# Rows of nine tokens, and the two heads of P side by side, in a thresholded attention with a maxout network behind it

## The chip, the core and the metric

The kernel runs on one core of one Trainium2 chip. A core has five engines that each work through their own list of instructions: TensorE (PE, matmuls; its weight loads are listed apart as PEld), VectorE (DVE), ScalarE (ACT), GpSimd (POOL) and SyncE (SP), which here only issues DMAs. Sixteen DMA engines move the data. The metric is the time of one execution on the device in microseconds (us). Lower is better.

## The reference, cut to what matters

```python
# q, k, v: (8 batches, 8 heads, 576 tokens, 64), float32; tau = 0.02
scores = q @ k.T / 8
thresh = max(scores, axis=-1) - tau
scores = where(scores >= thresh, scores, -1e9)
attn   = exp(scores - max(scores)); attn = attn / sum(attn)
x      = (attn @ v), heads side by side        # (4608 tokens, 512)
h      = maximum(x @ w1, x @ w2, x @ w3)       # 512 -> 768
out    = h @ w_out                             # (4608, 512), float32
```

Every token attends only to the keys whose score is within tau of the row's maximum. Then a maxout network with three input matrices is applied to each token.

## The kernel before, in words

**Tiling.** A batch has eight heads. Four heads are a *quad* (16 quads in all), in the code `g` or `L`; a quad is two *pairs*, `r` = 0 and 1, of two heads `i` each. A head's 576 tokens are 64 groups of nine; a load puts the group on the partition, so a partition holds tokens that follow each other in DRAM. For q and k one transfer brings tokens 0 to 7 of each group (`qm`, `km`: 16 token columns for two pairs) and another one, once per batch, token 8 of all eight heads (`q9`, `k9`, in `nine`). V comes as `vm` in two transfers per quad, four tokens of four heads each, and its ninth tokens in `v9`.

**Transposes and scores.** PE transposes q and k two token columns at a time (`couple`, `transposed`, tile `tp`); ACT or DVE copies the result into `qt` and `kt`, which hold 320 columns for pair 0 and 256 for pair 1. POOL makes `qs`, which is `qt` with its two row halves exchanged (`swapped`). `scores` makes 128 query rows by 576 keys of one head as two matmuls, each in one 64-row half of PE (tile `sc`). A *chunk* is 128 query rows of one head of each pair; its two steps are the two pairs. There are 9 chunks in a quad, 144 in all.

**Softmax.** For each step DVE finds the row maximum (`maximum`, tile `z`), ACT applies the threshold and the exponential (`exponents`, `numerators`), for some steps DVE masks instead of ACT (the digits 1 and 3 in `MASKED`). DVE takes the reciprocal of the two sums of a chunk (`reciprocals`, tiles `sm`, `rs`), and POOL multiplies and writes P in bfloat16 (`normalized`): step 0 into columns 0 to 575, step 1 into columns 576 to 1151. A DMA transpose (`turned`) turns P into `ptq`, nine blocks of 128 keys.

**Product.** `product` multiplies `ptq` by V (`vb`, V cast to bfloat16 by POOL in `cast_v`). Each pair accumulates in its own PSUM bank. Since P of the two steps follow each other, a block of 128 rows of `ptq` mixes keys: in a first half of the work each pair uses one row half of PE, and in the second half (letter `D` in the order, `issue(1)`) the row halves are exchanged. A gate, an empty instruction that waits for the end of the first half, stands between the two.

**Network.** `ffn` has 9 hidden pieces per batch with three matrices (tiles `ph`, `hm`, `hT`), and the output pieces (`po`, copied into `ob`). `outp` stores an `ob` of 128 rows with one DMA: 14 stores of 512 KB for pairs of token columns, 4 of 256 KB for the last batch; `ninth` stores the ninth tokens of two batches, 4 of 256 KB. These pieces use both row halves of PE and are cut in two in the same way (`halves`).

**Order.** Nothing is scheduled at run time. The string `ORDER` names each step by a letter, in one global order, and `_Ordered` ties every engine's instructions to that order. The letters that matter here: `l` a load, `t` a DMA transpose, `o` an output store, `i` a store of ninths, `S` scores, `T` transposes, `O` a product, `D` its second half, `F` and `B` the halves of a network piece, `p` one step of P, `r` a reciprocal, `y` a cast of V. A digit behind `S`, `T`, `O`, `F` names the PSUM slot. All DMAs but three at the start are issued from SP, in the order of their letters, so SP's queue carries loads, transposes of P and stores in one line. Buffers: six for P, two for `ptq`, two for `ob`, two for loaded q, k and V.

Line 100 of the kernel is the call inside `_Ordered`, so nearly all instructions of the profile stand under L100; they are told apart by their tiles.

Of the kernel before, what the change touches and what calls it, by code (L numbers as in the profile page):

```python
# [11 lines left out]
F32 = mybir.dt.float32  # L12
# [9 lines left out]
FLAT = 2.0 ** -100  # L22

MASKED = """
223222232233222220210000021233202222122020000010000001011211000010000131
101030100000110000000100000110000001001112002102100000103000100101000100
000001100101100010001000001100100001000101010001100000001000001000010001
100001110010001010010100000100010000100111000100100100000000010001010000
# [4 lines left out]
150605614372873482158427036045238761134628750738260415253670418765830142  # L33
123687540257136804843612507412875036125083746786120435601505613782473842
# [14 lines left out]
lllllllT3laT0qT2CT3laqClqS1qmyeS3S2mS0mS1gnlenelmT3mAS2zgqgeenT3kgymCT0llS1gAerT3qlqS0mqpcrnpeS2gnmS1lnmprtp  # L49
S3etemppzS0emS1nlktmS2nrpememyrkS3epS0epnS2pS1kntmrtmrmepeeS0S2mbsnmpnS3leS1pmrmepS2S3penmnmO10semsrkzDsS3wS  # L50
2pdwnT1S0rpmlpAlsmeT3etpteqnS1mT0nercpAS3ppeS2emtS0nnyelS1memgnqrekpnmmS3eO21kDT0tkrpmdwneqnS2etpqrppzwnS1tc
tlrS0F3plpmmeprnBelF2mHbzBgvepS1nS0nmT3S2rmaetmeS1mF3kBnptdpteeF0S1vrBmT2S3phpeS0cmmnypS2nrmpnS1nsmdrS3ggF0e
BmszespnlO12vebnpsrpDnS0wF3S1epwS2mgT0zatqmmetttrpBenvqsT1tF0pqS2BqcnF1S3hepksgeBS0mmnrsF2S3evmspmdlpS1mBdnr
evnS3pS0mpO12ebdnrplmnS3zeDenplmlwS0twtrympetS3eS1etypelmyF2S3kmrBnmklF1pF0selT3kkBBAuhF2rtS1peS3ventnBmF0S1
mBvtpdrF3kepS2plsnBqmrhmT1eCvdS0S2pplmreT1danmS3mpnS0mpS1edreppddqF2eqF3npmT0eBkncqBeS1vF0S2HerBmelnmvS3F2em
pT1prkBltaT0S3vCS1tmS2plpnemmT3adS0S1O23qrkepstenmeeDmS1pkkrkS0xS2psxF3rmmttnpS1msS0S2pedenrtekenttpBmmumdnp
S1S0S2trmyeO13pslmpdpT0emnlteekcDS2rslrplpwS0S1mxetdqqketF3F2mmeBBnS0hF1kT3sqBmndaF0vS3dltppvrS2pmnlS1mBleF3
endS2mBepnyHF1nrqmF0vBtdrrpS2vneT3psCpBS1mnetpteF3HS2mBF1meS0nseF2sBBkvS3emvqpdsryhtmpyS0F1S2eF3tnepnemrBBmS
0pnvrpyvO12seDpmnkdekrS0xweT3T2pmpnS1pS0CpAlmF3tdqmlS2rsBS0mF1pHsnmeS2qF3prntnoBopemvBdeS0nrpdF2pS1vS3mBeF0l
etmS1nByemhltdrptknmF2eT3BvptS1rvaemeS0mnpeeS3mtkpF2nkS0snF3sretS1merBmpkUS1erBmppplnS0eS1qmtdtunO23mkqoeeS1  # L60
eDmrS0pnwpT1mxT3yppdndS2CperN0nApmldT3pS1cemnF2qBjS3tBdrnlltqkmS1yeeF0mS3nseHmntrdBF1olvrpF2BepBhS0S3vlF1S2B
mepmmeS3T0vnlF2pdT1eBpaS0rpmCkvdS1teF3dmetlmS2BnpmnprS0F1kS2mmrhqBdS3epepnF0ntdF2dvBetmS1vBT3pmtqS0npS1rkdht
aO23mlrS0qppdeeenmeDkmS1xkrmF0wT2plBeF1vpCdlnS2rnneqBmvS3edtpplS0F2pS1mmmBtdrinpS3lhF0eT1mBpadneS3dypnkvF1em
S2rBlpmS0dF3vS2tneBmmpF1rpHS0qpT2ttneBmrsF3tnS0dCsBvmvS1mS2pemS0epetednemqnF3T1etBkT2lCnnArUpS1edmeS0eeO23np
rdS1pkmkmDprlwwF0S1deserlkmS2epBpymF1S3qBeqrukmkhtdpS2S0mtnptF1nmS3BeF2pmrnvndF0ltdBrpS3T1teavpBemS2F1pHeqmp
S3msrdpnF0qS2mpBlF3vneBBrddtenvhedF2S1S0BkS3etemF1lemvT0BpmyCnntpS2tF3F0llrvymppS1nskBsBhyprmpvtS2S1mmdT0S3n
lmS2epaerkO01pS3mmpsesesDnnqeF3lewrF2qBT0ewF1reCyvkBBplnF3HnvS0pS2neBmovF1T0ttmsprBknS3ladhpmpS2F0mS1odrleyB
tmnesF3ptplT2BtS1qepvS0CvmmS2S3ndmrenF1eS0nkprpeT2mBmS3AqrdmT0eplpnF2cS3S0skeuepemtS1rdnmBeS3mpknueqS1mN0npt
S2mBT3pstjdrmtS1prekmAO20pedqkerdnS1nDmS3pslprdxxmoS1T2eF0mS3epqncnelpBF1mtHnS2mprssttBF3pT0apveS2BF0S1rnmpe
vdBmS2eS3HlpF1dennmmyprS0meBqepvF2tS3BmF0lvS1F3mBtBkF2dnnehdS1pvF0temsBrT3dqentdBvrHpF1pCeS2myenBlnvtS3pyF0s  # L70
mS2pmkBnslO13S2rrvemDsppS2F0qlwntepeemewnF1BrtdpBokT3tnhvpleaS2S0eS1mF3S2emBtF0rnpdmmvS1eT2BF3msS1pltnBqkypr
ChdsF2mytS0BnrS1letvlmevnqS3pS0mpptmpmeF2edS3kertnpelsS1F0BmT3empnS1enlkkskrBupmaT2pcS3S1uqdrerO02pemeS3kDmn
snmS3tqrpppS1wxlenF0trS2dpmnemS3lBF1lpeypmlmS2dT3hopyklameBS0F2vsrS3pBpmtF1smeveS0nBF3mttntlheS2kremBdT0evF1
F2pBcpvF3BrkendhBestvS0F1nmT2kqrF3aBBehppvrpdtS2mdS0ntS3pmmF1peeeS2BmtvO03S2nndkpenS1rDxmpmS2F1wrT3mS0nqBtdc
F2pesprS3nqmS0BqenvpedmmphF1T3aBT2CS0tvS3qeT1psmnF2dnmrepoekAF0prBBhvF3nS1BmsqF2tveqS0dBdperqS1eS3ptepmvmnnp
S0F2T1CmmS3rkntS0S1esBmrpsntepmpumS3eF0tS2tmmpkS1erBdkenpUO23nDmekrxS0epoN1wsmpteS2BjmnpS3rF0seF2tBBhpmkdS1F
3nndF0ovtBrmS2S1veepmtBF3kS2edhBeemspmF0F1rnpBlF2vpsS3rnBevkdtS0mplBhF1dvrS3mnmeBnseF2F0neBvhS3rpppF1nBpBmpF
3nF2dBevnvHpS0eS1tsmrmF3BeS0isS1rnvmdeBF2evtmptF0ntBF3BpnshrBpS1enyekvS2vpS0mmdtF3ymS1mdrBpnerO20S1neeDuS3mp
xxtenpO21mkpstDrS3xwesS2mnF0iemstF1BpptoF2pBkF3BerpnsnurtF0enBHF1BvrhBpF2vF0ptpvBF1BBpvptptF2BHvvO13O20DxDF1
uxowwF2F0oF1UBhF2BF0vBvF3BoBF1F2BhBvHF3F0BvBvvN3F0F1UouBjoi  # L80
# [31 lines left out]
def kernel(  # L112
# [58 lines left out]
    nines = {}  # L171

    def nine(b):
        if b not in nines:
            nines[b] = {n: ld.tile([128, 6 if n == "v" else 4, D], F32, name=n + "9", bufs=1) for n in "qkv"}
        return nines[b]

    def load(g, first=False):
        b, qd = quads[g]
        L = Ls[g] = dict(b=b, qd=qd, first=first)  # L180
        for n in "qk":
            L[n] = ld.tile([128, 16, D], F32, name=n + "m")
        L["vm"] = ld.tile([128, 4, 4, D], F32, name="vm")

        def rows_of(src, heads):
            return src[b, heads].rearrange("(r i) (p c) d -> (i p) r c d", i=2, c=9)

        four = slice(4 * qd, 4 * qd + 4)
        q2 = nc.scalar if first else sync
        srcs = (("q", q, sync), ("k", k, q2))  # L190
        for n, src, e in srcs:
            if first:
                e.dma_start(out=L[n][:, 0:8], in_=rows_of(src, four)[:, 0, 0:8])
            else:
                e.dma_start(out=L[n].rearrange("p (r c) d -> p r c d", r=2), in_=rows_of(src, four)[:, :, 0:8])
            yield
        if qd == 0:
            for n, src, e in srcs:
                e.dma_start(out=nine(b)[n], in_=rows_of(src, slice(0, H))[:, :, 8])
                yield  # L200
        if first:
            for n, src, e in srcs:
                e.dma_start(out=L[n][:, 8:16], in_=rows_of(src, four)[:, 1, 0:8])
                yield
        for x in range(2):
            sync.dma_start(out=L["vm"][x:128:2].rearrange("p h c d -> p h (c d)"),
                           in_=v[b, four].rearrange("h (p c) d -> p h (c d)", c=9)[:, :, 256 * x:256 * x + 256])
            yield
        if qd == 0:
            for r in range(2):  # L210
                sync.dma_start(out=nine(b)["v"][64 * r:64 * r + 64],
                               in_=v[b, 2 * r:2 * r + 6].rearrange("h (p c) d -> p c h d", c=9)[:, 8])
                yield


    def cast_v(L):
        L["vb"] = vp.tile([128, 4, 4, D], BF16, name="vb")
        pool.tensor_copy(out=L["vb"], in_=L["vm"])
        yield
        if L["qd"] == 0:  # L220
            t = nine(L["b"])["vb"] = vp.tile([128, 2, 2, D], BF16, name="vb9", bufs=2)
            v9 = nine(L["b"])["v"]
            for a in range(2):
                pool.tensor_copy(out=t[:, a], in_=v9[:, 4 * a:4 * a + 2])
                yield

    def couple(L, n, r, j, rows=slice(0, 128)):

        if j == 4:
            t, f = nine(L["b"])[n], 2 * L["qd"]  # L230
        else:
            t, f = L[n], 8 * r + (0, 4, 2, 6)[j]
        return t[rows, f:f + 2, :].rearrange("p a d -> p (a d)")
# [26 lines left out]
    def transposed(L, n, r):  # L260
# [5 lines left out]
        def first(where):  # L266
            st["ps"] = ps = bank("tp", where)
            main = ps.rearrange("p (i z) -> p i z", i=2)[:, :, 0:256].rearrange("p i (jj u x) -> p i jj x u", jj=2, x=2)
            for j in range(nj):
                for i in (1, 0):  # L270
                    rows = slice(64 * i, 64 * i + 64)
                    tensor.transpose(main[:, i, j // 2, j % 2] if j < 4 else ps[:, 512 * i + 256:512 * i + 320],
                                     couple(L, n, r, j, rows), identf[rows, rows])
# [489 lines left out]
    x = 0  # L763
# [39 lines left out]
```

## Time and profile before

| | us |
|---|---|
| median of 3 runs | 450.48 (449.23 to 450.99) |
| the profiled execution | 445.24 |
| its span, first to last instruction | 443.5 |
| PE busy | 416.5 |
| ACT busy | 397.2 |
| DVE busy | 394.7 |
| POOL busy | 332.7 |

The granted clock of PE was 0.998. The busy times are sums over the whole span; they say which engine is nearly full, not who waits for whom. The views used below are: the page's busy shares and DMA part; the busy time of each engine in stretches; the waits (engine, what it waited for: us in total, times, longest); the chain of work that ended last in order of time; the groups of instructions (busy us, mean ns of one, idle before them); the DMA issues with their median time from issue to landing.

### The profile page before, as it was taken

The page shows a single profiled execution, that of the slowest core. Times are in us where ns is not written, and L with a number is a line of the kernel's source. Part 1 is how long each engine was busy: PE and PEld are TensorE (multiplying, and loading weights), DVE is VectorE, ACT ScalarE, POOL GpSimd, SP SyncE. Part 2 cuts the span into 40 slices and gives each one's busy share as a digit, 9 for nine tenths or more (in the row PEclk, how much of TensorE's full clock was granted, in tenths as well). Part 3 has the DMA queues.
Part 4 walks back from the last instruction along what each step waited for, and adds up shares of the span by engine and source line. Part 5 has one row for each costly group of instructions (what it writes and reads, how often), then busy time and mean ns, then how long its engine had stood idle before and what let it go on. Part 6 is the DMA issues. An engine that isn't in the chain of part 4 may idle for free.

```text
span 443.5 us, 15544 instructions
## 1 busy us (share of the span) xinstructions
PE 416.5 (94%) x5922; PEld 317.3 (72%) x5924; DVE 394.7 (89%) x1129; ACT 397.2 (90%) x808; POOL 332.7 (75%) x499
## 2 busy tenths in 40 slices
PE   7677698999999999999999999999998999999995
PEld 5434467666787868887687787878777887887862
DVE  3999799999999999999999999999999898997533
ACT  5999799889999999999999999999999897999321
POOL 3799889887998968898799689978686795647300
PEclk9999999999999999999999999999999999999999
DMA  9999999999999999999988999999999579869911
GB/s 267 359 227 199 235 276 201 216 210 204 193 255 145 251 216 242 222 195 221 201 144 159 294 234 207 184 237 212 163 213 200 130 104 204 156 98 134 213 49 71
DMA packets 211595, 88.05 MB, mean 199 GB/s; under 512 B 186944, under 2 KB 199744, under 8 KB 211520
## 3 DMA queue, kind: packets, MB, share of 16 engines
q1 hardware_dynamic: 210704, 86.40, 97.1%
q8 instruction: 46, 0.75, 0.7%
q10 hardware_dynamic: 816, 0.66, 0.5%
q14 instruction: 29, 0.24, 0.2%
HBM read 35.13 MB, written 9.44 MB: 100 GB/s over the span
## 4 chain that ended last, share of the span: by engine, by line
PE 58%; DVE 11%; POOL 10%; issue 7%; ACT 7%; DMA 5%; SPq 0%; POOLq 0%; DVEq 0%
PE ph L100 22%; PE sc L100 21%; POOL P L100 7%; PE po L100 6%; PE o L100 6%; DVE z L100 6%; ACT z L100 6%; DMA ptq<-P 3%; PE tp L100 3%; POOL qs L100 1%; DMA wo<-in_moe_w_dram 1%; DMA qm<-in_q_dram 1%; POOL th L100 1%; DVE stage L100 1%; DVE hm L100 1%
## 5 line engine op out<-in xcount | busy, mean ns | idle before, releaser
L100 POOL TENSOR_SCALAR P<-z,rs 128x576 bf16<-128x576 f32 x250 | 199.3, 807 | 38.3 <-DVE rs L100 16.9
L100 DVE TENSOR_SCALAR_CACHE_REDUCE z<-sc 128x576 f32<-128x576 f32 x250 | 182.6, 749 | 13.1 <-PE sc L100 6.0
L100 PE MATMUL sc<-kt,qt 64*128 64x256 f32 (+2 forms) x640 | 182.9, 423 | 5.2 <-ACT z L100 3.5
L100 PE MATMUL sc<-kt,qs 64*128 64x320 f32 (+2 forms) x640 | 181.0, 413 | 4.1 <-DVE z L100 2.0
L100 PE MATMUL ph<-xt,w 64*128 64x288 bf16 (+2 forms) x2304 | 172.5, 283 | 1.5 <-DVE stage L100 0.6
L100 PEld LDWEIGHTS <-w 64*128 64x128 bf16 x2304 | 131.0, 94 | 30.9 <-issue 4.8
L100 ACT ACTIVATE z<-z 128x576 f32<-128x576 f32 x178 | 119.8, 676 | 0.5
L100 ACT ACTIVATE z<-z,th 128x576 f32<-128x576 f32 x150 | 112.0, 766 | 2.0 <-POOL th L100 1.6
L100 PEld LDWEIGHTS sc<-kt,qs 64*128 64x128 f32 (+1 forms) x640 | 89.0, 176 | 20.2 <-DVE z L100 7.1
L100 PEld LDWEIGHTS sc<-kt,qt 64*128 64x128 f32 (+1 forms) x640 | 89.1, 176 | 19.6 <-ACT z L100 7.4
L100 DVE SCALAR_TENSOR_TENSOR z<-z 128x576 f32<-128x576 f32 x72 | 60.7, 850 | 0.0
L100 PE MATMUL po<-wo,hT 64*128 64x512 bf16 (+2 forms) x454 | 54.5, 354 | 0.8 <-DVE hm L100 0.4
L100 POOL COPY qs<-qt 64x640 f32<-64x640 f32 (+1 forms) x62 | 43.5, 701 | 12.0 <-ACT qt L100 6.7
L100 POOL TENSOR_SCALAR th<-nm 128x1 f32<-128x1 f32 x103 | 31.6, 306 | 25.8 <-DVE z L100 6.1
L100 PE MATMUL o<-ptq,vb 64*64 64x64 bf16 (+2 forms) x1296 | 45.4, 272 | 3.5 <-DMA ptq<-P 2.2
L100 ACT ACTIVATE z<-z,nm 128x576 f32<-128x576 f32 x63 | 47.6, 766 | 0.5 <-DVE z L100 0.5
L100 PEld LDWEIGHTS <-vb 64*64 64x64 bf16 x1296 | 32.8, 107 | 17.2 <-issue 5.5
L100 PEld LDWEIGHTS <-hT 64*128 64x128 bf16 (+1 forms) x456 | 30.7, 94 | 16.7 <-issue 2.1
L100 DVE TENSOR_TENSOR hm<-ph,hm 128x576 bf16<-128x576 f32 (+2 forms) x48 | 36.0, 750 | 6.2 <-PE ph L100 3.7
L100 DVE TENSOR_TENSOR hT<-ph,hm 128x576 bf16<-128x576 f32 (+2 forms) x48 | 36.1, 752 | 2.0 <-PE ph L100 1.1
L100 ACT ACTIVATION_READ_ACCUMULATOR z<-z 128x1 f32 x178 | 34.4, 193 | 0.0
L100 POOL TENSOR_SCALAR P<-stage,rs 128x576 bf16<-128x576 f32 x38 | 29.0, 769 | 3.6 <-DVE rs L100 1.2
(52 smaller groups left out, 409.3 us busy)
## 6 DMA issues: line engine op xcount, KB each, us to landing
vm<-in_v_dram SPq DMA_DIRECT2D x32, 256.0 KB, 4.2
qm<-in_q_dram SPq DMA_DIRECT2D x15, 512.0 KB, 4.9
km<-in_k_dram SPq DMA_DIRECT2D x15, 512.0 KB, 5.3
out_dram<-ob SPq DMA_DIRECT2D x14, 512.0 KB, 4.5
ptq<-P SPq DMA_TRANSPOSE x144, 4.5
v<-in_v_dram SPq DMA_DIRECT2D x16, 96.0 KB, 3.3
hT<-in_moe_w_dram SPq DMA_DIRECT2D x3, 512.0 KB, 9.2
stage<-in_moe_w_out_dram SPq DMA_DIRECT2D x3, 512.0 KB, 6.2
```

The costliest lines, as they stand in the source:

```text
L100: ins = fn(*a, **kw)
```

## The change

Five things change together.

1. **Loads.** q and k come as 9 tokens per group in one row of 2,304 bytes (`qm`, `km`: 18 columns), V as 9 tokens of two heads on 64 partitions, twice per quad (`vm`: 128 x 2 x 9 x 64). The transfers of ninth tokens and the tiles `q9`, `k9`, `v9`, `vb9` are gone. `l` goes from 98 to 68 letters.
2. **Key order.** A couple is now two neighbouring columns (`f = 2 * j + 10 * r`); the fifth couple of pair 0 takes its token 8 and token 0 of pair 1. Keys and queries are no longer interleaved by two in `kt` and `qt`; `KEYS` lists which token stands in which block.
3. **P and product.** `normalized` writes P in nine runs of 64 columns with a gap of 64 between them, so that every block of 128 columns holds 64 keys of each step. After the transpose each pair has its own row half of PE throughout; the exchange of halves, the gate and the letter `D` are gone.
4. **Reciprocals.** The sums of two chunks share a tile of four columns, and the new letter `R` (21 of them) takes four reciprocals at once.
5. **Stores, order, masks.** Output rows now stand as two blocks of 64 on the partitions, and the stores follow that. `ORDER`, `MASKED` and `TILES` are new: 92 masked steps in place of 81.

The core of the diff (the strings left out):

```diff
+KEYS = ((1, 3, 5, 7, 0, 2, 4, 6, 8), (0, 2, 4, 6, 8, 1, 3, 5, 7))
...
         for n in "qk":
-            L[n] = ld.tile([128, 16, D], F32, name=n + "m")
-        L["vm"] = ld.tile([128, 4, 4, D], F32, name="vm")
+            L[n] = ld.tile([128, 18, D], F32, name=n + "m")
+        L["vm"] = ld.tile([128, 2, 9, D], F32, name="vm")
...
+        heads = slice(4 * qd, 4 * qd + 4)
+        srcs = [(L[n].rearrange("p (r c) d -> p r (c d)", r=2),
+                 src[b, heads].rearrange("(r i) (p c) d -> (i p) r (c d)", i=2, c=9),
+                 scalar if first and n == "k" else sync) for n, src in (("q", q), ("k", k))]
+        if first:
+            for r, cols in ((0, slice(0, 9 * D)), (1, slice(0, D)), (1, slice(D, 9 * D))):
+                for dst, src, e in srcs:
+                    (sync if cols.start else e).dma_start(out=dst[:, r, cols], in_=src[:, r, cols])
+                    yield
+        else:
+            for dst, src, e in srcs:
+                e.dma_start(out=dst, in_=src)
+                yield
+        for r in range(2):
+            sync.dma_start(out=L["vm"][64 * r:64 * r + 64].rearrange("p i c d -> p i (c d)"),
+                           in_=v[b, 4 * qd + 2 * r:4 * qd + 2 * r + 2].rearrange("i (p c) d -> p i (c d)", c=9))
             yield
...
-    def reciprocals(c):
-        c["rs"] = small.tile([128, 2], F32, name="rs")
-        vector.reciprocal(c["rs"], c["sm"])
+    def reciprocals(c, steps):
+        vector.reciprocal(column_of(c, "rs", 0, 2 * steps), column_of(c, "sm", 0, 2 * steps))
...
-            pool.tensor_scalar(out=P[:, n * S:(n + 1) * S], in0=c["z", n],
-                                    scalar1=c["rs"][:, n:n + 1], scalar2=1.0, op0=OP.mult, op1=OP.mult)
+            pool.tensor_scalar(out=P.rearrange("p (j r k) -> p j r k", r=2, k=64)[:, :, n],
+                                    in0=c["z", n].rearrange("p (j k) -> p j k", k=64),
+                                    scalar1=column_of(c, "rs", n, n + 1), scalar2=1.0, op0=OP.mult, op1=OP.mult)
...
-        def issue(swap):
-            if swap:
-                gate = tensor.nop()
...
-            for m in range(last + 1):
-                for ms in zip(*(pieces_of(h ^ swap, h, m) for h in (1, 0))):
...
+            for j in range(9):
+                for ms in zip(*(pieces_of(r, j) for r in (1, 0))):
+                    for o, w, x in ms:
+                        tensor.matmul(o, w, x, start=(j == 0), stop=(j == 8))
...
-                    dst = rows_out[:, 0:8].rearrange("p (x c) m -> p x c m", x=2)[:, :, c:c + 2]
+                    dst = rows_out[:, 2 * c:2 * c + 4].rearrange("p (u a) m -> u p a m", u=2)
                     stores.append(lambda: sync.dma_start(out=dst, in_=ob))
...
-                stores.append(lambda: sync.dma_start(out=rows_out[:, c:8:4], in_=ob))
+                t0 = 4 * (c // 2) + c % 2
+                stores.append(lambda: sync.dma_start(out=rows_out[:, t0:t0 + 3:2].rearrange("p u m -> u p m"), in_=ob))
```

In the two stores `rows_out` has the 64 groups `p` of a batch as its first dimension; the old destination keeps `p` first, the new one puts the two blocks `u` first.

More of the change, by code (lines that the diff above doesn't have):

```diff
@@ L54 @@
[L54 to L58, printed above, removed]
@@ L79 @@
[L79 to L80 removed]
+lllllT2lllT0lAqqT1CT2algqglS0CqS2mS3emT1egaS0glkyqlmemS2T1mqdneS3ncT2mzAS0znqmS1qRmpzpeeepT2pS3nckegltmrntpe
+S0kpS1myS2nrmS3epempktetmS0nS2emenrS1npS0pkmrS3mtemS2leprpmplengpmS1msS0nmS2enrpnegmS1mdS3pseemreO02wpzptewS
+0eS2kmnmT1kenArdtzT2pcT3AntS0mqS2tpT1nrrCS3etS1meeS0lmpmgppeqdO21lpqkmknnwS0tsS3ewnF1RmmeS2BtF3sS0pBmpnHF2nr
@@ L81 @@
+1BhBpF0svS2BS1S3trnemvmpedF2pkF0S1BdynemBF3mehvdporkF2BS0pS1vBhmpF3mF0nreBkevntpBtS2srvmS1neptS3dtmemF0S2mpB
+ynekS3smupO12nxO03twrxipskxeeS2S1nF0pF3dttmrmpdF2epF1nBertBettkprUphnBvBnpF3odrpvtenF0BBF2tF1HrpvBpBF3tHF0pv
+BBpO21xvxvF3tuO01F3wxF2F0oBhBF1F2uBvF3F0BBvHvF1BBF2vF3HBvBvN3F1oUooF0Buoji
 """
@@ L168, in bank @@
         return ps_s.tile([128, 1024], F32, name=name, tag=f"s{where}")
[L171 to L176, printed above, removed]
     def load(g, first=False):
@@ L181, in load @@
         for n in "qk":
-            L[n] = ld.tile([128, 16, D], F32, name=n + "m")
-        L["vm"] = ld.tile([128, 4, 4, D], F32, name="vm")
[L185 to L195, printed above, removed]
-            yield
@@ L197, in load @@
[L197 to L213, printed above, removed]
+            L[n] = ld.tile([128, 18, D], F32, name=n + "m")
[4 more added lines that the diff above has]
+                 scalar if first and n == "k" else sync) for n, src in (("q", q), ("k", k))]
@@ L216, in cast_v, with couple @@
     def cast_v(L):
-        L["vb"] = vp.tile([128, 4, 4, D], BF16, name="vb")
+        L["vb"] = vp.tile([128, 2, 9, D], BF16, name="vb")
         pool.tensor_copy(out=L["vb"], in_=L["vm"])
         yield
[L220 to L233, printed above, removed]
+    def couple(L, n, r, j, rows):
+        f = 2 * j + 10 * r
+        return L[n][rows, f:f + 2, :].rearrange("p a d -> p (a d)")
@@ L271, in first @@
                     rows = slice(64 * i, 64 * i + 64)
-                    tensor.transpose(main[:, i, j // 2, j % 2] if j < 4 else ps[:, 512 * i + 256:512 * i + 320],
-                                     couple(L, n, r, j, rows), identf[rows, rows])
+                    at = 512 * i + 64 * j
+                    tensor.transpose(ps[:, at:at + 64], couple(L, n, r, j, rows), identf[rows, rows])
         def done(e):
@@ L294, in scores @@
                 i, c = (0, idx) if idx < 4 else (1, idx - 5)
-                t = L["qt"] if c % 2 == x else L["qs"]
-                off = 320 * r + 128 * (c // 2)
+                t = L["qt"] if (c + r) % 2 == x else L["qs"]
+                off = 128 * (c // 2) + (0, 0, 256, 320)[2 * r + c % 2]
                 tensor.matmul(ps[:, cols], t[rows, i, off:off + 128], L["kt"][rows, i, kc],
@@ L300, in scores @@
                 for i in range(2):
-                    t = L["qt"] if r == x else L["qs"]
-                    tensor.matmul(ps[64 * i:64 * i + 64, cols], t[rows, i, 256:320],
+                    t, off = L["qt"] if r == x else L["qs"], 256 * (1 + r)
+                    tensor.matmul(ps[64 * i:64 * i + 64, cols], t[rows, i, off:off + 64],
                                   L["kt"][rows, i, kc], start=True, stop=True)
@@ L352, in numerators, with column_of @@
             scalar.activation(out=z, in_=z, func=AF.Exp, scale=-1.0 / FLAT, accum_out=acc)
-    def reciprocals(c):
-        c["rs"] = small.tile([128, 2], F32, name="rs")
-        vector.reciprocal(c["rs"], c["sm"])
+    columns = {}
+    def column_of(c, name, a, b):
+        pair, at = c["n"] // 2, 2 * (c["n"] % 2)
+        if (name, pair) not in columns:
+            columns[name, pair] = small.tile([128, 4], F32, name=name)
+        return columns[name, pair][:, at + a:at + b]
+    def reciprocals(c, steps):
+        vector.reciprocal(column_of(c, "rs", 0, 2 * steps), column_of(c, "sm", 0, 2 * steps))
     def normalized(c):
@@ L375, in product @@
     def product(L, target, part=None):
-        pt, vb, vrb = L["pt"], L["vb"], nine(L["b"])["vb"]
-        st, mine = {}, []
+        pt, vb = L["pt"], L["vb"]
+        st = {}
         b = L["b"]
@@ L390, in product, with pieces_of @@
         cols = slice(at, at + hi - lo)
-        def pieces_of(r, h, m):
-            rows = slice(64 * h, 64 * h + 64)
+        def pieces_of(r, j):
+            rows = slice(64 * r, 64 * r + 64)
             for *qs, p0, w in runs:
                 for i in range(2):
-                    v_ = vb[rows, 2 * r + i, (1, 3, 0, 2)[m], :] if m < 4 else vrb[rows, L["qd"], i, :]
-                    yield (st[r][64 * i:64 * i + 64, p0:p0 + w], v_,
-                           pt[rows, 4 if m == 4 else m + 5 * r, qs[i]:qs[i] + w])
-        def issue(swap):
-            if swap:
-                gate = tensor.nop()
-                tc.add_manual_dep(gate.ins, mine[0], mybir.DependencyInfo(mybir.DependencyClass.Sync, mybir.DependencyReason.DATA), reason="swap")
-            last = 3 if swap else 4
-            for m in range(last + 1):
-                for ms in zip(*(pieces_of(h ^ swap, h, m) for h in (1, 0))):
-                    for o, w, x in ms:
-                        ins = tensor.matmul(o, w, x, start=(not swap and m == 0), stop=(swap == 1 and m == last))
-            mine.append(ins.ins.name)
+                    yield (st[r][64 * i:64 * i + 64, p0:p0 + w], vb[rows, i, KEYS[r][j], :],
+                           pt[rows, j, qs[i]:qs[i] + w])
         def first(*where):
@@ L413, in first @@
                 st[r] = bank("o", where[r])
-            issue(0)
+            for j in range(9):
+                for ms in zip(*(pieces_of(r, j) for r in (1, 0))):
+                    for o, w, x in ms:
+                        tensor.matmul(o, w, x, start=(j == 0), stop=(j == 8))
         def done(r):
@@ L423, in done @@
             return run
-        return _Piece((L["b"], L["qd"], part), first, lambda: issue(1), [done(r) for r in range(2)])
+        return _Piece((L["b"], L["qd"], part), first, None, [done(r) for r in range(2)])
     def copied(e, dst, src):
@@ L699, in issue @@
             p.first(*where)
-            halfway.append(p)
-        elif what == "D":
-            p = halfway.pop(0)
-            p.second()
             line["x"].extend(p.done)
@@ L729, in issue @@
             c, r = line[what].pop(0)
-            if "sm" not in c:
-                c["sm"] = small.tile([128, 2], F32, name="sm")
-            else:
-                c["summed"] = True
+            c["summed"] = c.get("summed", 0) + 1
             numerators(c, r)
-        elif what == "r":
-            c = made[line["r"].append(0) or len(line["r"]) - 1]
-            assert c["summed"]
-            reciprocals(c)
-            line["p"].append(c)
+        elif what in "rR":
+            steps = 2 if what == "R" else 1
+            cs = made[len(line["r"]):len(line["r"]) + steps]
+            assert len(cs) == steps and all(c["summed"] == 2 for c in cs)
+            assert steps == 1 or cs[0]["n"] % 2 == 0
+            reciprocals(cs[0], steps)
+            line["r"].extend(cs)
+            line["p"].extend(cs)
         elif what == "t":
```

67 lines of the change are left out of this document (33 added, 34 removed).

## Prediction

> **What bounds the kernel now.** I read the page's busy shares first, then the DMA part and the busy times by stretch, then the waits and the chain that ended last.
>
> ```profile
> span 443.5 us, 15544 instructions
> PE 416.5 (94%) x5922; PEld 317.3 (72%) x5924; DVE 394.7 (89%) x1129; ACT 397.2 (90%) x808; POOL 332.7 (75%) x499
> ...
> DMA packets 211595, 88.05 MB, mean 199 GB/s; under 512 B 186944, under 2 KB 199744, under 8 KB 211520
> ...
> q1 hardware_dynamic: 210704, 86.40, 97.1%
> ```
>
> PE is busy for 416.5 of 443.5 us. The second thing to see is the last row: the packets of SP's queue took 97.1% of the span as a mean over 16 DMA engines. By stretch (columns: PE, PEld, DVE, ACT, POOL busy, clock, DMA share, GB/s):
>
> ```profile
> 0.00:115.00 115.00, 96.57 (x1220) 65.72 (x1222) 101.66 (x304) 104.06 (x214) 93.99 (x131) 1.00 1.06 239
> 115.00:415.00 300.00, 297.17 (x4326) 236.69 (x4324) 282.19 (x811) 289.21 (x588) 238.66 (x369) 1.00 1.02 195
> 415.00:443.50 28.50, 22.76 (x384) 14.89 (x380) 10.84 (x16) 3.97 (x7) 0.02 (x1) 0.97 0.30 79
> ...
> 10.00:12.00 2.00, 0.82 (x6) 0.28 (x3) 2.00 (x7) 1.97 (x6) 1.04 (x1) 1.00 1.05 383
> 260.00:280.00 20.00, 20.00 (x294) 15.68 (x292) 19.49 (x62) 19.68 (x41) 18.48 (x27) 1.00 1.21 221
> ```
>
> From 115 to 415 us PE misses 2.8 us in 300: the bound there is PE. The DMA engines stand beside it with a share of 1.02 and, in the busiest twenty microseconds shown, 1.21 (a share can pass 1 because packet times overlap). 383 GB/s is the fastest stretch I found, 23.9 GB/s for one of 16 engines.
>
> ```profile
> PEld L100 <- DMA ptq<-P: 2.5, 2, 1.5
> PEld L100 <- PE o L100: 2.3, 7, 0.4
> PE o L100 <- DMA ptq<-P: 2.2, 3, 1.2
> POOL P L100 <- DMA ptq<-P: 1.5, 2, 1.0
> ...
> 338.06 4.24 DMA ptq<-P
> 342.34 1.21 PE o L100 x18
> ...
> 363.77 4.51 DMA ptq<-P
> 368.32 1.44 PE o L100 x20
> ...
> 415.05 4.52 DMA ptq<-P
> 419.61 2.02 PE o L100 x104
> ```
>
> PE waits for transposed P only 4.7 us in all (2.5 and 2.2), but three times the chain runs straight through the landing of a transpose into a product. So the products have hardly any slack: a transpose that lands late is PE time lost.
>
> **The change part by part.**
>
> The output stores. In the kernel before, a store of a pair of token columns writes DRAM as 64 groups x 2 blocks of 4 KB; after, as 2 blocks x 64 groups of 4 KB. The source keeps its 128 partitions. The number, size and content of the rows are the same.
>
> ```profile
> out_dram<-ob SPq DMA_DIRECT2D x14, 512.0 KB, 4.5
> ptq<-P SPq DMA_TRANSPOSE x144, 4.5
> ...
> out_dram<-obr SPq DMA_DIRECT2D x4, 256.0 KB, 2.6
> out_dram<-ob SPq DMA_DIRECT2D x4, 256.0 KB, 2.4
> ```
>
> Every transfer of the kernel before has a slowest dimension of 64 or 128 on both sides, which 16 engines divide evenly. The new stores alone have one of 2, so no row can price them. If the share-out still reaches 16 engines, they take 4.5 us as now. If each block goes to one engine, two engines carry 262,144 B each, at 23.9 GB/s 11.0 us, where now every engine carries 32,768 B in 1.4 us. I take the second end: with two blocks at the top there is nothing else to deal out, and this one transfer differs from all the others in just that. [...]
>
> No engine waits for a store soon: its buffer is wanted again a store later. But SP's queue carries everything else too. 13 of the 14 pair stores stand ahead of the last transpose in the new order; the first is its 728th of 2,756 entries, 26% of the way, about 117 us. So engines 0 and 1 of the split (say) get 13 x (11.0 - 1.4) = 125 us more in what is now the stretch from 115 to 415 us, and all 16 shares of a transpose have to land before its product starts.
>
> The loads. The ninth tokens came in 256 B rows of their own: 8 batches x (2 x 512 for q, k and 768 for V) = 14,336 packets; they now ride in rows of 2,304 B. V's 8,192 rows of 1 KB become 4,096. That is 18,432 packets fewer. The mean packet of the page is 0.971 x 443.5 us x 16 / 210,704 = 32.7 ns, so 18,432 x 32.7 / 16 = 38 us per engine over the run, less the bytes of the ninths (3.67 MB / 16 at 23.9 GB/s = 10 us): -28, of it 5/8 (batches 3 to 7) behind 115 us: -17 us. On 16 evenly loaded engines this would be worth 0 to the 4.7 us of PE's transpose waits; I take 2.
>
> Engines 0 and 1 in the middle stretch, then: 300 x 1.02 - 17 + 125 = 414 us of packet time. At the share of 1.02 that takes 406 us; at 1.21 it takes 342; by bytes alone (12.2 GB/s x 300 us + 13 x 229,376 B = 6.64 MB at 23.9 GB/s) 278, which would fit. I take 342, the greatest share a stretch has shown, since these two queues will never run dry: +42 us, with 0 and +106 as ends.
>
> The tail.
>
> ```profile
> 416.45 9.20 SPq L100 DMA_DIRECT2D out_dram<-ob  x3
> ...
> 425.12 14.72 SPq L100 DMA_DIRECT2D out_dram<-ob  x3
> 440.07 0.41 SPq L100 DMA_DIRECT2D out_dram<-obr  x1
> ...
> 437.38 0.69 DVE L100 COPY ob<-po 128x512 f32<-128x512 f32 x1 [1.89 <-PE po L100]
> 438.68 0.60 ACT L100 ACTIVATE ob<-po 128x512 f32<-128x512 f32 x1 [8.58 <-PE po L100]
> ```
>
> The last pair store, four single stores and the ninth's follow the last transpose. On two engines a single store has 131,072 B per engine, 5.5 us for now 0.7. The last two can be issued only at 438.1 and 439.3 us, when their copies end: 438.1 + 2 x 5.5, then the 2.6 us of the ninth's store, 451.7 where 443.5 is the end now (+8.2). With the pair store and the first two singles still queued from about 420 us on, it is 420 + 11 + 4 x 5.5 + 2.6 = 455.6 (+12.1). I take +10 us.
>
> PE. The program has as many matmuls as before (1,296 for the products, 1,280 scores, 576 transposes of q and k), and each row half works beside the other as before. The gates between a product's two halves go, 20 of them: the row of PEld waiting for o has 2.3 us, all of it gained at best; I take -2.3.
>
> POOL, DVE and ACT.
>
> ```profile
> L100 POOL TENSOR_SCALAR P<-z,rs 128x576 bf16<-128x576 f32 x250 | 199.3, 807 | 38.3 <-DVE rs L100 16.9 <-issue 4.6 <-ACT qt L100 3.6
> L100 POOL COPY qs<-qt 64x640 f32<-64x640 f32 x31 | 23.1, 746 | 9.7 <-ACT qt L100 6.0 <-DVE qt L100 1.9
> L100 POOL CAST vb<-vm 128x1024 bf16<-128x1024 f32 x16 | 17.1, 1069 | 0.4
> ...
> L100 DVE SCALAR_TENSOR_TENSOR z<-z 128x576 f32<-128x576 f32 x72 | 60.7, 850 | 0.0
> L100 ACT ACTIVATE z<-z 128x576 f32<-128x576 f32 x178 | 119.8, 676 | 0.5
> L100 ACT ACTIVATION_READ_ACCUMULATOR z<-z 128x1 f32 x178 | 34.4, 193 | 0.0
> L100 DVE RECIPROCAL rs<-sm 128x2 f32<-128x2 f32 x144 | 22.2, 157 | 1.8 <-ACT z L100 1.2
> ```
>
> P is now written in nine runs of 64 instead of one of 576. Nearest is the copy into qs, two runs of 320: 746 ns for 640 elements, no dearer per element than V's cast in one run (1,069 for 1,024). I take 0; 10% more, 0.08 us x 288 = 23 us of POOL, would still leave it (332.7 + 23) far under the span. Eleven masked steps move from ACT to DVE: DVE 11 x 850 ns = +9.4 us and their read-outs, ACT 11 x (676 + 193) = -9.6. 144 reciprocals become 102 plus 21 of double width: DVE -21 x 157 ns = -3.3; the first chunk of such a pair waits for the second, and with it POOL's two P steps, 21 x 0.8 us = 17 at most of the 111 us that POOL is idle. The other regroupings nearly cancel; POOL's thresholds and three weight casts add some 3 us. DVE about 396, ACT 388: none becomes the bound, cover is PE, so 0.
>
> The order and the start. Every step stands elsewhere in the new order, and no row prices that one by one. The most an order can gain is PE's idle time, 443.5 - 416.5 = 27 us, of it 2.8 in the middle; what it can lose is open. I take 0. At the start the first transposes need 288 KB of q and one more token of 32 KB, before 256 KB and the ninths' 128 KB: 64 KB less at 383 GB/s, 0.2 us, not counted.
>
> Sum on the profiled execution: 443.5 + 42 + 10 - 2.3 = 493.2 us of span, with the 1.7 us that lie around it (445.24 - 443.5) 494.9. The profiled run is 5.2 us under the median of 450.48; I leave that for the range.
>
> **The rivals.**
>
> Two engines, but hidden: the bytes would fit (278 us), and if transposes overlap the long rows freely only the tail is paid: 445.2 + 10 - 2.3 = 453 us, 458 against the median. For it: a share of 1.21 cost PE nothing at 260 to 280 us. Against it: the chain's three steps through a transpose, and the stores would take 9.9 GB/s (2.98 MB in 300 us) of the 11.7 that an engine has to spare at its best rate, in one queue with the transposes.
>
> The other side, the stores stay on 16 engines. Then the change does what its loads say: -2.3 for the gates and -2 for transposes that land earlier, 445.2 - 4 = 441 us, faster. It decides at one place: the first pair store lands in 4.5 us, not in 11 or more.
>
> P's nine runs are dear on POOL: from 0.38 us more each (288 x 0.38 = 109 us on 332.7) POOL passes the span and sets it; at 0.5 us, 480 us with the stores on 16 engines. Only the two-run copy speaks on it, and against.
>
> **How the numbers follow.** Two engines that set the pace 0.70, two engines hidden 0.10, sixteen engines 0.13, POOL 0.04, a worse order alone 0.03 (about 455). The time is the first one's, 495; its own range, 468 to 528: below, stalls that overlap; above, a share of 1.12 midway between 1.02 and 1.21 (414 / 1.12 = 370 us, +70), and the 5 us of the median. The range reaches down to the hidden case, 453, and leaves out the sixteen-engine case and the far end of the first. A measurement tells about 0.5% from no change: faster 0.11 and same 0.03 are the sixteen-engine case and its edge, slower 0.86.
>
> **What would show it.** Right: a pair store from issue to landing at 11 us or more; the median of 144 transposes well over 4.5; PE and PEld idle for ptq in tens of us; POOL waiting for P's buffers; a mean DMA share under 0.9 while the kernel waits for DMA, because 14 engines idle; over 8 us between the last copy into the output buffer and the end. Wrong: stores at 4.5 us. The sum fails in size if engines 0 and 1 take transposes between long rows faster than a share of 1.21, or if the new order leaves more room between a quad's last transpose and its product than the old one.

## The result and the profile after

The changed kernel takes 544.17 us (median; 541.6 to 546.39), the kernel before 449.86 us beside it: ratio 1.2135, 95% interval 1.2078 to 1.2192. It is slower by 94 us. The forecast was slower, 495 us, within 453 to 528: the direction and the cause (two engines for a store) hold, the size is half of what came, 45 us against 94.

The page after (busy shares, granted clock in 40 slices, DMA queue, the chain by engine and by line):

```profile
span 543.3 us, 15455 instructions
PE 436.4 (80%) x5921; PEld 330.3 (61%) x5924; DVE 398.9 (73%) x1106; ACT 392.2 (72%) x788; POOL 337.4 (62%) x499
...
PEclk8988999999897999969999979988889998899696
...
DMA packets 192685, 87.51 MB, mean 161 GB/s; under 512 B 172132, under 2 KB 176740, under 8 KB 192612
...
q1 hardware_dynamic: 192324, 86.20, 102.4%
...
PE 41%; DMA 21%; issue 10%; POOL 9%; ACT 7%; DVE 7%; SPq 3%; POOLq 0%; DVEq 0%
DMA ptq<-P 16%; PE ph L100 15%; PE sc L100 15%; POOL P L100 6%; PE po L100 5%; ACT z L100 5%; PE o L100 5%; DVE z L100 4%; SPq L100 3%; DMA qm<-in_q_dram 2%; DMA stage<-in_moe_w_dram 2%; PE tp L100 2%; POOL qs L100 1%; POOL w L100 1%; ACT stage L100 1%
```

The same two lines of the chain before:

```profile
PE 58%; DVE 11%; POOL 10%; issue 7%; ACT 7%; DMA 5%; SPq 0%; POOLq 0%; DVEq 0%
PE ph L100 22%; PE sc L100 21%; POOL P L100 7%; PE po L100 6%; PE o L100 6%; DVE z L100 6%; ACT z L100 6%; DMA ptq<-P 3%; PE tp L100 3%; POOL qs L100 1%; DMA wo<-in_moe_w_dram 1%; DMA qm<-in_q_dram 1%; POOL th L100 1%; DVE stage L100 1%; DVE hm L100 1%
```

Transposes in flight made 3% of a chain of 443.5 us (13 us) and make 16% of 543.3 us (87 us): that is most of the loss in one row. DVE, ACT and POOL are busy as long as before. PE is busy 20 us longer with the same matmuls, and its granted clock is lower: 0.922 as a mean, 0.998 before.

Where a store stands in SP's queue it can be read directly. First the kernel before around one pair store, then the changed kernel around one, then around two in a row (start, us, what):

```profile
293.20 0.94 SPq L100 DMA_DIRECT2D out_dram<-ob  x1
294.49 1.63 SPq L100 DMA_TRANSPOSE ptq<-P  x1
```

```profile
415.98 0.60 SPq L100 DMA_DIRECT2D out_dram<-ob  x1
416.69 9.67 SPq L100 DMA_TRANSPOSE ptq<-P  x1
...
212.27 1.24 SPq L100 DMA_DIRECT2D out_dram<-ob  x2
213.83 27.01 SPq L100 DMA_TRANSPOSE ptq<-P  x5
```

The store itself is issued in 0.6 us as ever. The transpose behind it then holds SP for 9.67 us instead of 1.63, and behind two stores five transposes take 27 us. What that does to the engines (same columns as in the prediction), and what moves while nothing but a store runs, in the tail:

```profile
200.00:220.00 20.00, 19.79 (x304) 15.69 (x302) 18.68 (x53) 19.22 (x41) 18.42 (x28) 1.00 0.64 136
220.00:240.00 20.00, 9.41 (x112) 7.29 (x108) 9.63 (x26) 8.73 (x20) 7.95 (x14) 0.83 0.99 94
...
510.00:517.00 7.00, 6.67 (x115) 4.69 (x117) 0.68 (x2) 1.36 (x3) 0.00 (x0) 0.77 0.14 46
```

From 220 to 240 us all engines stand for half of the time, at a clock of 0.83. And the last row says how many engines carry a store: a DMA share of 0.14 of 16 is 2.2 engines, 46 GB/s in all, 23 for each, so a store of 524,288 B takes 11.4 us.

The trace also holds landing records, a note of each share of a transfer that has landed; the views above do not print them one by one. A pair store of the kernel before has sixteen, the last 3.2 to 6.2 us after its issue began. A pair store of the changed kernel has one after about 1 us and then just two, together, after 12.8 to 14.4 us (22.2 for the second of two in a row). The transposes issued right behind such a store have all sixteen, 12.4 to 15.9 us after their issue began (24.0 behind two stores). Before, the slowest of the 144 took 8.6 us.

The waits for transposes, after:

```profile
POOL P L100 <- DMA ptq<-P: 30.1, 6, 11.3
PE o L100 <- DMA ptq<-P: 17.1, 8, 8.9
ACT ob L100 <- DMA out_dram<-ob: 7.0, 2, 4.9
PEld L100 <- DMA ptq<-P: 2.1, 2, 1.9
```

PE waits 17 us for P's transposes (2.2 before; PEld's row is largely the same waits seen a second time), but POOL waits longer still, 30 us (1.5 before): its six P buffers are full of blocks that have not left.

### The profile page after: what moved, and what is told of

Same layout as the page of the kernel before. It is cut to its first block, busy times and chain, and to the rows that moved or that the text cites. A ratio compares the mean times of both kernels' runs of the same rounds, so it can differ in the third digit from the quotient of the medians.

```text
span 543.3 us, 15455 instructions
## 1 busy us (share of the span) xinstructions
PE 436.4 (80%) x5921; PEld 330.3 (61%) x5924; DVE 398.9 (73%) x1106; ACT 392.2 (72%) x788; POOL 337.4 (62%) x499
## 3 DMA queue, kind: packets, MB, share of 16 engines
q1 hardware_dynamic: 192324, 86.20, 102.4%
## 4 chain that ended last, share of the span: by engine, by line
PE 41%; DMA 21%; issue 10%; POOL 9%; ACT 7%; DVE 7%; SPq 3%; POOLq 0%; DVEq 0%
DMA ptq<-P 16%; PE ph L100 15%; PE sc L100 15%; POOL P L100 6%; PE po L100 5%; ACT z L100 5%; PE o L100 5%; DVE z L100 4%; SPq L100 3%; DMA qm<-in_q_dram 2%; DMA stage<-in_moe_w_dram 2%; PE tp L100 2%; POOL qs L100 1%; POOL w L100 1%; ACT stage L100 1%
## 5 line engine op out<-in xcount | busy, mean ns | idle before, releaser
L100 PE MATMUL ph<-xt,w 64*128 64x288 bf16 (+2 forms) x2304 | 182.7, 291 | 28.1 <-issue 26.1
L100 PE MATMUL sc<-kt,qt 64*128 64x320 f32 (+2 forms) x640 | 189.2, 443 | 18.3 <-DVE z L100 11.4
L100 PE MATMUL sc<-kt,qs 64*128 64x256 f32 (+2 forms) x640 | 187.4, 430 | 14.9 <-ACT hm L100 6.0
L100 PEld LDWEIGHTS sc<-kt,qt 64*128 64x128 f32 (+1 forms) x640 | 96.5, 185 | 33.8 <-DVE z L100 14.8
L100 PEld LDWEIGHTS sc<-kt,qs 64*128 64x128 f32 (+1 forms) x640 | 96.8, 186 | 30.7 <-POOL qs L100 7.1
L100 ACT ACTIVATE z<-z 128x576 f32<-128x576 f32 x169 | 113.8, 675 | 0.3
L100 DVE SCALAR_TENSOR_TENSOR z<-z 128x576 f32<-128x576 f32 x81 | 67.3, 835 | 0.1
L100 POOL TENSOR_SCALAR th<-nm 128x1 f32<-128x1 f32 x116 | 34.9, 301 | 33.9 <-DVE z L100 14.2
L100 PEld LDWEIGHTS <-vb 64*64 64x64 bf16 x1296 | 33.7, 113 | 32.6 <-issue 25.0
L100 ACT ACTIVATE z<-z,nm 128x576 f32<-128x576 f32 x68 | 51.2, 765 | 1.4 <-DVE z L100 1.4
L100 ACT ACTIVATE hm<-ph 128x576 bf16<-128x576 f32 (+2 forms) x34 | 22.0, 647 | 40.8 <-PE ph L100 40.7
```

What stands on the lines that cost most here:

```text
L100: ins = fn(*a, **kw)
```

## The experiments

### Is it the stores? The changed kernel with other stores, the kernel before with the new ones

The changed kernel, each store cut in two DMAs:

```diff
-dst = rows_out[:, 2 * c:2 * c + 4].rearrange("p (u a) m -> u p a m", u=2)
-stores.append(lambda: sync.dma_start(out=dst, in_=ob))
+def store():
+    for u in range(2):
+        sync.dma_start(out=rows_out[:, 2 * c + 2 * u:2 * c + 2 * u + 2], in_=ob[64 * u:64 * u + 64])
+stores.append(store)
```

> The changed kernel with each output store cut into two DMAs of 64 rows, so that the slowest dimension of both sides is 64 again; nothing else differs. Theory A (the two-block store on two engines makes the whole loss, because SP stands about 8 us at the next transpose behind each of 14 stores): 440 to 455 us, and the transpose behind a store is issued in about 2 us instead of 9.4. Rival B (the new order or the new loads make a good part of it; the changed kernel was already some 8 us late before its first store): 458 to 480 us. Rival C (the stores hardly matter): over 520 us.

451.84 us against 449.17: ratio 1.0077 (1.0045 to 1.0110). 92 of the 94 us are gone. Theory A.

The kernel before with the two blocks first (single stores likewise):

```diff
-dst = rows_out[:, 0:8].rearrange("p (x c) m -> p x c m", x=2)[:, :, c:c + 2]
+dst = rows_out[:, 0:8].rearrange("p (x c) m -> x p c m", x=2)[:, :, c:c + 2]
```

> The kernel before with the two-block destination alone: the same rows of the output, the two blocks first. The rows within a store land in another order, so the output is permuted. Theory A: 14 pair stores x about 7 us of SP standing + about 9 us at the tail = 535 to 560 us. Rival B (in an order with room behind its stores the two engines are hidden): 453 to 480 us. Rival C (the destination's dimensions do not matter): 450 us.

551.46 us, ratio 1.2274 (1.2210 to 1.2338): +102 us. Two letters exchanged in a destination give the whole loss, and a little more, in a kernel that has nothing else of the change. Theory A again; B and C fall.

### How much of it is the tail?

The same edit, in the last batch's single stores and the last pair store alone.

> The kernel before with the two-block destination only in the four single stores of the last batch and the last pair store, which follow the last transpose (rows within these stores permuted). Theory A (the tail's two engines have 11 + 4 x 5.5 us to carry from about 420 us): 457 to 463 us, +8 to +12. Rival B (the tail is hidden under PE's last work): 450 to 453 us.

457.55 us, ratio 1.0194 (1.0127 to 1.0261): +8.4 us. The tail is not hidden and has the size that was forecast for it. What is left of the 102 us, 94, belongs to 13 stores before the last transpose: 7.2 us each.

### A pace or a price for each store? Fewer stores, and four engines

The two-block destination in the odd batches alone (`if b % 2`), 6 stores:

> The kernel before with two-block pair stores in the odd batches alone: 6 of 14, rows within a store permuted, the tail's stores as they were. Theory D: the two-block kernel lost 102 us, 8 of it in the tail, so 94 / 13 = 7.2 us for a store, 6 x 7.2 = 43 us: 487 to 498 us. The prediction's step: (306 + 6 x 9.6) at a share of 1.21 is 301 us: 450 to 456 us.

492.30 us, ratio 1.0972 (1.0920 to 1.1023): +43.7 us, 7.3 for each of the six. The prediction's step had these six hidden; they are paid like the thirteen.

The count alone would also fit a pace at a lower share: about 1.07 to 1.11 in the place of 1.21 gives the 43.7 and the 94 us as well (an estimate, with 10.0 us more per store). The trace says where the time goes. This run has the order of the kernel before, so each step that writes P (288 of them on POOL) can be laid beside the same step there. Up to 176 us they are 3.0 to 3.5 us late, two stores on 16 engines included. Behind the two-block stores at 167.6 and 186.6 us they are 20.3 to 20.8 us late, and stay so from 207 to 299 us, through two more stores on 16 engines. Behind the next two (287.8 and 321.8 us) it is 32.6 to 34.2 us, behind the last two 45 to 46.5. The loss falls behind the stores that two engines carry; between them nothing is added and nothing is won back. A reason that fits is in the prediction's own table: PE misses 2.8 us in 300 there, so it has no time to make up.

The pair stores as four blocks of 32 groups:

```diff
-dst = rows_out[:, 0:8].rearrange("p (x c) m -> p x c m", x=2)[:, :, c:c + 2]
+dst = rows_out[16 * c:16 * c + 32, 0:8].rearrange("p (u a) m -> u p a m", u=4)
```

> The kernel before with each pair store written as 4 blocks of 32 groups (the same 128 rows of 4 KB, permuted), so that the slowest dimension is 4; the single stores stay as they were. On four engines a store takes 5.5 us instead of 11. Theory D (each store is paid whole: SP stands at the next transpose until the few engines have drained, and nothing else moves): per store some 2.5 to 3.5 us, 14 of them: 480 to 500 us. The prediction's step (the engines are only a pace that can overlap: (306 + 14 x 4.1) us at a share of 1.21 is 300 us, what the stretch takes anyway): 450 to 456 us.

517.88 us, ratio 1.1544 (1.1498 to 1.1590): +69 us, 4.95 for each of 14 stores (5.3 if the last, behind the last transpose, costs nothing). The prediction's step falls again, and theory D was too low by 18 us. A reason is in the tail of that run, where one store runs alone:

```profile
491.00:497.00 6.00, 5.55 (x112) 3.87 (x113) 0.89 (x2) 0.63 (x2) 0.00 (x0) 0.62 0.26 68
```

0.26 of 16 is 4.2 engines, so four it is, but they move 68 GB/s together, 17 each where two engines had 23. A store takes 524,288 B / 68 GB/s = 7.7 us and not 5.5. Beyond the 1.4 us of a store on 16 engines that is 6.3 us more, of which 4.95 are paid; on two engines 10.0 more, of which 7.2 are paid. In both some 70 to 85% of the extra time of a store becomes time of the kernel. (The 1.4 us are the prediction's estimate from its best rate.) The landing records agree: four late ones for each pair store, the last after 10.0 to 11.8 us (15.3 for the second of two in a row).

### SP's queue, or the two engines?

The pair stores of the two-block kernel issued from ACT (`scalar.dma_start`), its four single stores left as before, and as a control the pair stores of the kernel before.

> The kernel before with the two-block pair stores issued from ACT's queue instead of SP's (rows within a store permuted; the tail's single stores as they were). Theory D1 (the loss is SP standing: a transpose behind the store cannot be issued while two engines' lists are full): with the stores on another queue SP goes on, 455 to 500 us, and the transpose issued next behind a store takes its usual 1.3 to 3 us. Theory D2 (the loss is that two engines are occupied, and a transpose has shares on them whatever the queue): 520 to 550 us.

> Control for the last run: the kernel before with its own destination pattern and its pair stores issued from ACT's queue. 446 to 454 us: ACT spends some 14 x 0.6 us on issuing and may wait for five copies of DVE.

542.91 us (ratio 1.2169, 1.2121 to 1.2217), +96.7; the control 448.83 (1.0048, 1.0008 to 1.0088). Another queue saves nothing that matters: D2. SP's queue in that run, beside a store that ACT issued at 327.4 us:

```profile
328.00 2.58 SPq L100 DMA_TRANSPOSE ptq<-P  x1
330.63 0.62 SPq L100 DMA_DIRECT2D v<-in_v_dram  x1
331.34 14.26 SPq L100 DMA_TRANSPOSE ptq<-P  x3
```

The first transpose now gets through, the next ones stand all the same. That SP stands is how the loss shows, not its root. The root shows in the landing records of loads: a q load that SP issued 0.2 us after ACT had issued a store (at 202.4 us) has fourteen of its sixteen shares after 2.9 us and the last two after 10.4. In the run with stores on four engines a load of V behind a store (at 175.9 us) has twelve after 3.1 us and four after 10.9, and all nine loads so placed there lack just four. So such a load waits for the engines that have a store to write, whichever queue the store came from. Not everything is as plain: with two-block stores some loads, of q above all, and nearly all transposes have all sixteen shares late together, and why is open.

### Would a better place for the store hide it?

In the order of the kernel before, each pair store was moved to the place right behind the last transpose of a quad; with two blocks (the four single stores too), and as a control with the destination as it was. Eleven of the fourteen stand there; three, in the last batch's two quads, stand behind the transposes of a part of a quad.

> The kernel before with two-block stores (rows within a store permuted) and each of the 14 pair stores moved in the order to the place right behind the last transpose of a quad, so that no product waits for the next transposes for some 20 us. Theory E1 (the loss is paid where a product waits for a late transpose): the moved stores are mostly hidden, 455 to 500 us, and PE's waits for ptq fall under 10 us. Theory E2 (the loss is paid by the steps that feed P: six P buffers fill while SP stands, POOL stands, then DVE and PE): 525 to 555 us wherever the store is.

> Control for the last run: the kernel before with its own destination pattern and the stores at the moved places. 446 to 452 us: where a store of 1.4 us stands matters little.

561.79 us (ratio 1.2553, 1.2466 to 1.2640); the control 452.23 (1.0098, 1.0068 to 1.0127). E1's forecast falls: the loss is not smaller. E2's figure of 525 to 555 us was passed by 7. Its mechanism is only half shown, for the waits went elsewhere:

```profile
PEld L100 <- DMA ptq<-P: 23.1, 2, 14.2
PE o L100 <- DMA ptq<-P: 22.6, 2, 14.1
PE tp L100 <- DMA qm<-in_q_dram: 21.2, 7, 7.2
ACT ob L100 <- DMA out_dram<-ob: 19.5, 2, 9.9
POOL P L100 <- DMA ptq<-P: 13.6, 3, 8.0
DVE ob L100 <- DMA out_dram<-ob: 10.0, 1, 10.0
```

POOL's wait for P's buffers is smaller than after the change. PE's and PEld's first rows are the same two waits, of 9 and 14 us, so the edit did not free the products of all waiting: the first came where the last transpose, issued just ahead of a store, had twelve of its sixteen shares land with the store; the second behind one of the three stores inside a quad. But 23 us at products are a small part of 110. PE also waits 21.2 us for loads of q (4.6 in the control), and copies wait 29.5 us for an output buffer whose store has not landed (1.6 in the control). So the loss is not tied to products: a delay of some 10 us finds a buffer that is not deep enough, here P, there q's or the output's. More P buffers would have been a direct test; no run tried it.

### What is the rest of the change worth?

The changed kernel with the old destination pattern, whole stores:

```diff
-dst = rows_out[:, 2 * c:2 * c + 4].rearrange("p (u a) m -> u p a m", u=2)
+dst = rows_out[:, 0:8].rearrange("p (x c) m -> p x c m", x=2)[:, :, c:c + 2]
```

> The changed kernel with the destination pattern of the kernel before (64 groups first), one DMA per store; its rows are in another order on the partitions, so the output's rows are permuted. Theory A: 445 to 452 us; if cutting the stores in two cost something in the run before, this one is faster than its 451.8. Rival B (the new loads, the product or the order cost what is left): 451 to 455 us, no faster than that run.

The same with `ORDER`, `MASKED` and `TILES` of the kernel before:

> As the last one, with the order, masks and tiles of the kernel before: what loads in rows of nine, P in nine runs and the product without a gate are worth by themselves; the output's rows are permuted. If they gain what the prediction gave them (2.3 for the gates, 2 for the loads): 444 to 447 us. If they cost: 450 to 456 us.

And the changed kernel with the old order and stores in two DMAs:

> The changed kernel's loads, key order, P in runs and product, with the order, masks and tiles of the kernel before (letters of the transfers and halves that are gone are left out) and the stores in two DMAs of 64 rows. Theory A (loads, P and product cost nothing in themselves): 440 to 452 us. Rival B (the new loads or product are dearer): over 455 us, as e1. If e1 is slower than this run, the difference is the new order.

With the new order 448.91 us, ratio 1.0009 (0.9979 to 1.0039): no difference. With the old order 450.76, ratio 1.0046 (1.0020 to 1.0072), slower by half a per cent; with cut stores on top 454.72, ratio 1.0107 (1.0036 to 1.0177). So loads in rows of nine, P in runs and a product without a gate gain nothing that these runs show. That the order made for them takes back a cost is not shown: the two runs with whole stores differ by less than their noise.

Set beside the first run (451.84 us), the changed kernel with whole stores (448.91) is 0.7% better, each against its own kernel before; with the old order it is 0.6%, inside the noise of four runs. So cutting a store in two seems to cost something there. The profiled executions are less clear: 3 of the 6.7 us between their spans lie ahead of the first store, where the two programs are the same. The kernel before with cut stores:

```diff
-stores.append(lambda: sync.dma_start(out=dst, in_=ob))
+def store():
+    for x in range(2):
+        sync.dma_start(out=rows_out[:, c + 4 * x:c + 4 * x + 2], in_=ob[x:128:2])
+stores.append(store)
```

> The kernel before with each store cut into two DMAs of 64 rows on every second partition. If the cut itself is what separates the changed kernel with cut stores (451.8) from the one with whole stores (448.9): 450.5 to 453 us. If not: 447.5 to 450.

447.47 us, ratio 1.0017 (0.9979 to 1.0055): there it costs nothing that shows. Both halves have 64 rows; in the kernel before they stand on every second partition, in the changed kernel on 64 neighbouring ones. The issues of the two runs, kernel before first, changed kernel second:

```profile
out_dram<-ob SPq DMA_DIRECT2D x28, 256.0 KB, 3.3
```

```profile
out_dram<-ob SPq DMA_DIRECT2D x28, 256.0 KB, 4.3
```

The same 256 KB in 3.3 and in 4.3 us (3.9 in the changed kernel with the old order). The 128 KB singles at the end, where little else moves, have 2.1 and 2.4. That the partitions make the difference is not shown: the two cuts were not compared in one kernel. V's loads have moved in the same way, from every second partition to 64 neighbouring ones. That this is why the new loads gain nothing is not shown: with whole stores they land in 4.7 us for 288 KB, before in 4.2 for 256 KB, about the same for each byte.

## Why the prediction was right or wrong

- **Two engines for the new stores: right**, and priced right: 11.0 us said, 11.4 from the tail's 46 GB/s, 12.8 to 14.4 from issue to landing. The slowest dimension of the destination was the sign, before any run; that it sets the number of engines was then the author's estimate, and the tails here and of the run with four blocks bear it out: 2.2 engines where it is 2, 4.2 where it is 4.
- **The middle stretch: wrong, by a factor of two.** The step that failed is "414 us of packet time ... at 1.21 it takes 342: +42 us". It takes the extra 125 us for load that spreads over the stretch and overlaps at the best share seen. The runs show a price for each store instead: 7.2 or 7.3 us in the kernel before, whether there are 13 or 6, and 86 us in all here (94 less the tail's 8.4), 6.6 for each of 13. With six stores that sum leaves the stretch at its 300 us, and the six were paid all the same, each where it stands. What spoke against the step stood in the prediction's own first part: a chain that runs straight through the landing of a transpose, and a PE that misses 2.8 us in 300, leave no slack into which a load could spread. (PE's own slack was smaller than the 4.7 us named there: that adds PEld's and PE's rows, which are mostly the same waits.)
- **Clock.** The prediction had no term for it. In the tail, below (same columns), PE is busy for 0.07 us of 504 to 509 us; its granted clock is 0.50 there and still 0.50 from 511 to 513 us, where PE is busy throughout, and 1.00 from 514 us on. The mean clock of the profiled runs is 0.985 to 0.998 in those with no such store, 0.959 with six, 0.922 here, and the same matmuls are busy 436.4 instead of 416.5 us.

```profile
504.00:509.00 5.00, 0.07 (x4) 0.10 (x5) 0.00 (x0) 0.60 (x1) 0.00 (x0) 0.50 1.22 190
511.00:513.00 2.00, 2.00 (x49) 1.50 (x43) 0.33 (x1) 0.36 (x1) 0.00 (x0) 0.50 0.18 43
514.00:520.00 6.00, 6.00 (x88) 4.16 (x88) 1.77 (x3) 1.19 (x2) 0.00 (x0) 1.00 0.14 56
```

- **The tail: right.** +10 us said, +8.4 measured by itself.
- **Gates and loads: nothing came.** -2.3 us for the gates and -2 for earlier transposes were forecast, the second for the sixteen-engine case, 441 us. That case has now been run, and gives 448.91 against 448.56. The row that stood for the gates counted waits of PEld; with whole stores that row is gone, and the time is not.
- **P in nine runs: right.** POOL's mean is 797 ns for the 250 steps, 807 before; for the other 38 steps it is 817 and 769, so the 288 together take as long as before.
- **What would show it: four of six.** Stores that land after 11 us or more, the waits of PE and POOL for ptq and the long end (13.6 us between the last copy and the end) were there. The transposes' median did not rise as forecast: only those close behind a store are late, and the view has 4.5 us in both (before, after). For the changed kernel that view knows the landings of just 22 of the 144; by the landing records the median is 4.9 us, and 14 take over 10.

```profile
DMA to landing us min/median/max: 3.2/4.5/8.6
```

```profile
DMA to landing us min/median/max: 3.2/4.5/15.2
```

- The mean DMA share did not fall under 0.9 either. It went from 97.1% to 102.4% while the rate fell from 199 to 161 GB/s: almost the same bytes of this queue (86.2 MB, 86.4 before) now have 556 us of packet time per engine where they had 431, so the time of a packet must hold time in which it stands. The rate would have been the sign to name.

## What to carry to other kernels

Look at the slowest dimension of what a DMA writes: here two engines of 16 carried the whole store where it was 2 (a DMA share of 0.14 in the tail, 46 GB/s), and four where it was 4 (0.26, 68 GB/s), and loads behind them waited for their shares on those engines (a q load's last two shares came after 10.4 us, the other fourteen after 2.9). Price such a transfer one by one, as a stop of what is queued behind it, and not as load on an engine, as soon as the chain of work runs through a transfer's landing: here 7.2 us for each of 13 stores and 7.3 for each of six. If a transfer must be cut in halves, try every second partition as well as neighbouring halves: the landings here favour the first, 3.3 us against 4.3 for 256 KB, though no run isolates it.

## What the runs showed that was not expected

- Four engines moved 68 GB/s together where two moved 46: 17 GB/s for each against 23. Why is open.
- A transpose behind such a store is held at its issue, 9.67 us, so SP's time in a DMA instruction shows a congestion that the median from issue to landing hides (4.5 us in the view, unchanged).
- A q load issued 0.2 us after a store had fourteen of its sixteen shares after 2.9 us and the last two only after 10.4; the transposes right behind a store have all sixteen late together, 12.4 to 15.9 us after their issue began.
- The same 256 KB took 4.3 us from 64 neighbouring partitions in the changed kernel and 3.3 us from every second one in the kernel before.
- The granted clock fell to 0.83 in a stretch where PE waited for data (220 to 240 us), and the mean of the run to 0.922. PE's busy time grew by 20 us, its idle time by 80.
